# Gated linear attention and a low-rank mixer: two more batches in whole chunks, orders from a table, and the last batch's transposes on a DMA queue

## The chip, the cores and the metric

The kernel runs on one core of one Trainium2 chip. The metric is the device time of one execution, in microseconds; a kernel's time is the median over its runs. The engines are named as in the profile: PE (TensorE matmul), PEld (its weight loads), DVE (VectorE), ACT (ScalarE), POOL (GpSimd) and SP (SyncE, here the queue that issues DMA transfers).

## The reference

For 4 batches, 8 heads, 768 time steps and head dimension 48, a gated state is carried along time, and its output goes through a low-rank token mixer and an MLP:

```python
for t in range(S):                                   # S = 768, state is D x D per head, D = 48
    state = alpha[:, :, t, :, None] * state + np.einsum('bhd,bhe->bhde', k[:, :, t], v[:, :, t])
    y[:, :, t] = np.einsum('bhd,bhde->bhe', q[:, :, t], state)
x = y.transpose(0, 2, 1, 3).reshape(B, S, H * D)     # 4 x 768 x 384
h = x.transpose(0, 2, 1) @ U @ V                     # U: 768 x 32, V: 32 x 768
u = x + h.transpose(0, 2, 1)
out = u + np.maximum(u @ w_ch1, 0.0) @ w_ch2         # 384 -> 1536 -> 384
```

Inputs and output are float32; the kernel computes in bfloat16 with float32 sums.

## The kernel before

Each batch has three parts. The first computes the attention, in six units of 128 rows. Within a unit the decay is a running product of alpha: `lt` is the logarithm of alpha (ACT), a triangular matmul sums it along time into a PSUM bank, and two exponentials on ACT give `ai` (its inverse) and `aa`; a small third one gives `tot`, the decay over the whole unit. `rk = k * ai` and `rq = q * aa` are made on DVE or GpSimd, `rv` is a cast of v. PE transposes `rk` and `rq` (into PSUM, from where ACT or DVE copies them to `kT` and `qT`), multiplies them into scores, DVE masks the scores into `pm`, and PE adds the state's share (`qT` by the state `st`) to `pm` by `rv`. The result is copied to `xb`. The next state is made from `rk` by `rv`, the last state and `tot`.

There are two forms of unit. `stage_pair` (batches 0, 1 and 2, by `PAIR`) takes two chunks of 128 time steps together, but half of the heads: even and odd steps lie next to each other on a partition, so that a load (L342) moves runs of 96 floats. It works on blocks of 64 rows, with 16 small matmuls for the scores (L445), 16 for the masked product (L531), 8 for the state (L479), 4 for the state's share (L518), 8 transposes (L418) and 8 matmuls for the cumulative sum (L384 to L391). `stage_gla` (batch 3) takes one whole chunk of 128 steps and all heads: its load (L349) moves runs of 48 floats; it has 8 matmuls for the scores (L605), 8 for the masked product (L664), 4 for the state (L628), 4 for the state's share (L662), 8 transposes (L584) and 6 for the cumulative sum (L554 to L557).

The second part, `stage_mix`, applies the low-rank mixer (L681, L712) and transposes the result (L722) to `uT`. The third is the MLP: `mlp1` (L749, three matmuls of 384 columns per group, then a relu on ACT, L759, or DVE, L761, into `h1t`) and `mlp2` (L772, then an addition on DVE, L779, and a store, L780). The MLP of a batch is interleaved with the attention of the next one. At the start PE also runs matmuls on a tile of zeros (L291), wherever it would wait in the first 28 us.

The order is made when the program is built. Every step is recorded with `P.add`, with the engines that may run it and a cost for each, what it reads and writes, a priority, and a `slack`. `Plan.run` then simulates the engines with these costs and picks, step by step, the one that can start first; ties go by priority. It also hands out the buffers: input tiles come from a pool of 36 (`io`), and matmul results from the eight PSUM banks. What comes out is a fixed order for each engine. All transfers are issued on SP's queue: 96 input loads of 192 KB (four tensors, 24 units), 24 weight tiles (L317), two small ones and 24 stores. They take eight completion semaphores in turn, and a transfer is issued only when the one eight places before it has landed.

Of the kernel before, what the change touches and what calls it, by code (L numbers as in the profile page):

```python
# [11 lines left out]
ALU = mybir.AluOpType  # L12

# [23 lines left out]
class Op:  # L37
    __slots__ = ("engs", "fn", "prio", "deps", "bufs", "n", "users", "est", "i", "mode", "slack", "eng", "t")


class Plan:
# [4 lines left out]
    TOL = 150.0  # L46
# [10 lines left out]
    def add(self, engs, fn, r=(), w=(), prio=0.0, mode="F", slack=0.0, after=()):  # L57
        op = Op()
        op.engs, op.fn, op.prio, op.mode, op.slack = engs, fn, prio, mode, slack
# [17 lines left out]
        op.deps.discard(op)  # L77
        bufs = []
# [10 lines left out]
    def run(self):  # L89
        for op in self.ops:  # L90
            op.n = len(op.deps)
            for d in op.deps:
                d.users.append(op)
        ready = [op for op in self.ops if op.n == 0]
        clock = {}
        order = []
        dma = 0.0
        mode = "F"
        todo = len(self.ops)
        while todo:  # L100
            per = {}
            for op in ready:
                t = op.est
                for b in op.bufs:
                    if b.slot is None:
                        s = sorted(x for x in b.pool.free if x is not None)
                        if len(s) <= b.reserve:
                            t = None
                            break
                        t = max(t, s[b.reserve])  # L110
                if t is None:
                    continue
                at = {eng: max(t, clock.get(eng, 0.0)) for eng in op.engs}
                soon = min(at[eng] + c for eng, c in op.engs.items()) + self.TOL
                for eng, c in op.engs.items():
                    if at[eng] + c <= soon:
                        per.setdefault(eng, []).append((at[eng], op))
            best = None
            for eng, ok in per.items():
                t0 = min(t for t, _ in ok)  # L120
                t1, op = min(((t, o) for t, o in ok if t <= t0 + 1.0), key=lambda x: (x[1].prio, x[1].i))
                key = (t1, t1 + op.engs[eng])
                if best is None or key < best[0]:
                    best = (key, eng, op)
            if best is None:
                raise RuntimeError("the plan is stuck")
            (t, _), eng, op = best
            for b in op.bufs:
                if b.slot is None:
                    p = b.pool  # L130
                    _, x = min((f, x) for x, f in enumerate(p.free) if f is not None)
                    p.free[x] = None
                    b.idx, b.slot = x, p.slots[x]
            ready.remove(op)
            op.eng, op.t = eng, t
            cost = op.engs[eng]
            if eng == "SP":
                dma = max(dma, t + 600.0) + cost
                clock[eng] = max(t + 450.0, dma - 3500.0)
                end = dma + 2000.0  # L140
            else:
                if eng == "PE" and op.mode != mode:
                    cost += self.SWITCH
                    mode = op.mode
                clock[eng] = end = t + cost
            order.append(op)
            done = end + self.LAT[eng]
            for b in op.bufs:
                b.left -= 1
                b.last = max(b.last, done)  # L150
                if b.left == 0:
                    b.pool.free[b.idx] = b.last
            for u in op.users:
                u.n -= 1
                if eng == "PE" and "PE" in u.engs:
                    u.est = max(u.est, end)
                else:
                    u.est = max(u.est, done + u.slack)
                if u.n == 0:
                    ready.append(u)  # L160
            todo -= 1
        self.order = order
        self.clock = clock
        at = self.warm_from
        for op in order:
            if op.eng == "PE" and op.t < self.warm_until:
                n = int((op.t - at - 100.0) * self.warm_share / 216.0)
                for _ in range(n):
                    self.warm()
            if op.eng == "PE":  # L170
                at = op.t + op.engs["PE"]
            op.fn(op.eng)
# [7 lines left out]
def kernel(  # L180
# [33 lines left out]
    PAIR = (0, 1, 2)  # L214
    RES = (1, 1, 1, 0)
    P = Plan()
# [42 lines left out]
    nc.vector.memset(offd[64:128, :, 0], -30000.0)  # L259

# [54 lines left out]
    def weight(dst, src, key, prio, pr, engs):  # L315
        t = Buf(io)
        P.add({"SP": 540.0}, lambda e: nc.sync.dma_start(flat(t), src), w=[t], prio=prio)  # L317
# [17 lines left out]

    def stage_loads(b):
        def load(t, src, c, key):
            if b in PAIR:
                hs, sl = slice((c % 2) * HP, (c % 2 + 1) * HP), slice((c // 2) * 2 * C, (c // 2 + 1) * 2 * C)
                P.add(  # L340
                    {"SP": 750.0},
# [7 lines left out]
            P.add({"SP": 1000.0}, lambda e: nc.sync.dma_start(t(), src[b, :, sl, :].rearrange("h t d -> t h d")), w=[t], prio=key)  # L349

        for c in range(NC):
# [3 lines left out]
            for t, src, o in ((at, alpha, -0.7 if c else 0.0), (kt, k, 0.1), (qt, q, 0.2), (vt, v, 1.25 if c < NC - 1 and b in PAIR else 0.3)):  # L355
                load(t, src, c, kk + o)

    def xk(b, xb, c):
        return [(xb, c, 0), (xb, c, 1)] if b in PAIR else [(xb, c)]

    def stage_pair(b, u, sprev, xb):
# [3 lines left out]
        sl = 0.0 if b == 0 else 150.0  # L365
# [9 lines left out]
        P.add({"ACT": 435}, lambda e: nc.scalar.activation(jh(lt()[:, :, 0:D]), raw(at), AF.Ln), r=[at], w=[lt], prio=pr + 40, slack=sl)  # L375
        rv = Buf(rvs)
        P.add({"POOL": 480, "ACT": 420}, lambda e: copy(e, jh(rv()), raw(vt)), r=[vt], w=[rv], prio=pr + 20, slack=sl)
# [18 lines left out]
        P.add({"PE": mm(DM, Q, Q, 8, 4, 4, 4, 4)}, f_cum, r=[lt], w=[cb], prio=pr + 30, slack=sl)  # L396
        aa, ai, tot = Buf(aas), Buf(ais), Buf(tots)
        P.add({"ACT": 390}, lambda e: nc.scalar.activation(ai().rearrange("t h d -> t (h d)"), cb()[:, 0:DM], AF.Exp, scale=-1.0), r=[cb], w=[ai], prio=pr + 20, slack=sl)  # L398
        P.add({"ACT": 390}, lambda e: nc.scalar.activation(aa().rearrange("t h d -> t (h d)"), cb()[:, 0:DM], AF.Exp), r=[cb], w=[aa], prio=pr + 21, slack=sl)  # L399
        P.add({"ACT": 100}, lambda e: nc.scalar.activation(tot()[:, :, 0], cb()[:, DM : DM + 8], AF.Exp), r=[cb], w=[tot], prio=pr + 22, slack=sl)  # L400
# [7 lines left out]
        P.add(both, lambda e: f_scale(e, rk, kt, ai), r=[kt, ai], w=[rk], prio=pr + 10, slack=sl)  # L408
        P.add(both, lambda e: f_scale(e, rq, qt, aa), r=[qt, aa], w=[rq], prio=pr + 11, slack=sl)
# [20 lines left out]
        P.add({"PE": mm(*[C] * 4)}, lambda e: f_tr(rk, tk), r=[rk], w=[tk], prio=pr + 18, slack=sl)  # L430
        P.add({"PE": mm(*[C] * 4)}, lambda e: f_tr(rq, tq), r=[rq], w=[tq], prio=pr + 18, slack=sl)
        P.add({"DVE": 335, "ACT": 500}, lambda e: f_ev(e, kT, tk, False), r=[tk], w=[kT], prio=pr + 8, slack=sl)
        P.add({"DVE": 600, "ACT": 500}, lambda e: f_ev(e, qT, tq, True), r=[tq], w=[qT], prio=pr + 8, slack=sl)
# [17 lines left out]
        P.add({"PE": mm(*[C] * 4)}, f_sc, r=[kT, qT], w=[sc[0], sc[1]], prio=pr + 10, mode="Q", slack=sl)  # L451
# [6 lines left out]
        for par in range(2):  # L458
            P.add({"DVE": 605}, lambda e, par=par: f_mask(par), r=[sc[par]], w=[(pm, par)], prio=pr + 5, slack=sl)
# [26 lines left out]
        if onpe and sprev is not None:  # L486
            P.add({"PE": mm(Q)}, lambda e: f_id(e, 0, False), r=[(sprev, 1)], w=[db[0]], prio=pr + 8, slack=sl)
        P.add({"PE": mm(*[2 * D] * 4)}, f_d, r=[rk, rv], w=db, prio=pr + 8, mode="H", slack=sl)
        for c in range(nch):
# [10 lines left out]
            if onpe or prev is None:  # L500
                if onpe and c == 1:
                    P.add({"PE": mm(Q)}, lambda e: f_id(e, 1, True), r=[(st, 0)], w=[db[1]], prio=pr + 7, slack=sl)
                P.add({"DVE": 270}, lambda e, c=c, f=f_st: f(e, db[c]()[:, 0:Q]), r=[db[c], tot], w=[(st, c)], prio=pr + 4, slack=sl)
            else:
# [4 lines left out]
                    r=[db[c], prev], w=[sm], prio=pr + 4, slack=sl,  # L509
                )  # L510
                P.add({"POOL": 480, "DVE": 270}, lambda e, sm=sm, f=f_st: f(e, sm()[:, 0:Q]), r=[sm, tot], w=[(st, c)], prio=pr + 4, slack=sl)
# [24 lines left out]
        P.add({"PE": mm(*[2 * D] * 4, *[D] * 8) + 95}, f_y, r=[qT, rv, (pm, 0), (pm, 1)] + [x for x in before if x is not None], w=[yb[0], yb[1]], prio=pr, mode="H", slack=sl)  # L536
        for c in range(2):
            P.add({"ACT": 250, "DVE": 265}, lambda e, c=c: copy(e, xb()[:, 2 * blk + c, half * Q : (half + 1) * Q], yb[c]()[:, 0:Q]), r=[yb[c]], w=[(xb, 2 * blk + c, half)], prio=pr, slack=sl)
        return st

    def stage_gla(b, c, sprev, xb):
        kk = b * NC + c
        pr = kk * 100.0
        sl = 150.0
# [288 lines left out]
```

## Time and profile before

| | |
|---|---|
| time, median of 3 runs | 177.71 us (177.3 to 178.09) |
| span of the profiled execution | 175.2 us, which is 2.5 us under the median of the runs |
| PE busy | 165.0 us, 94% |
| DVE, ACT, POOL busy | 116.8, 104.9 and 52.9 us |
| PE clock granted | 1.000 throughout |
| chain that ended last, by engine | PE 62%, SP's queue 14%, DMA 14%, POOL 4% |
| loads, issue to landing | 4.5 us median (L342), 4.6 us (L349) |

How to read it: the span runs from the first to the last instruction of one profiled execution, and what lies around it is the difference to the time of a run. Busy time counts an engine's instructions, not its issuing of transfers. The chain that ended last is followed back from the last instruction, at each step to what released it. Rows of a line give durations as min/median/max. A mean of a matmul is its latency; how densely matmuls follow each other is read from the chain.

### The profile page before, as it was taken

What the parts mean: (1) busy time and instruction counts of PE and PEld (TensorE: products, weight loads), DVE (VectorE), ACT (ScalarE), POOL (GpSimd) and SP (SyncE); (2) the same over time, 40 slices, a digit from 0 to 9 for tenths busy, and PEclk for the clock granted to TensorE, in tenths of its full rate; (3) what the DMA queues carried; (4) which work ended last, traced back from release to release, by engine and by line L of the source; (5) the groups of instructions that cost most, each with busy time, mean ns of one, the idle gap of its engine ahead of it and who ended that gap; (6) DMA issues with size and microseconds to landing.
All of it is one profiled execution on the core that took longest, in us unless ns stands there. A gap on an engine that the chain in (4) does not pass through costs nothing.

```text
span 175.2 us, 5094 instructions
## 1 busy us (share of the span) xinstructions
PE 165.0 (94%) x1990; PEld 104.8 (60%) x1990; DVE 116.8 (67%) x251; ACT 104.9 (60%) x248; POOL 52.9 (30%) x92
## 2 busy tenths in 40 slices
PE   7788998699999999999999999999999999999992
PEld 2455665366566775766666666766666566666660
DVE  4588785398998889979888649987373385000321
ACT  4588874678788966457677434647784110996000
POOL 8055366258234432233243242920331000000000
PEclk9999999999999999999999999999999999999999
DMA  5999999999999999999698991021000212100222
GB/s 131 275 248 258 256 277 329 256 300 329 272 258 269 256 283 282 272 175 242 151 202 141 206 178 46 4 89 45 4 0 0 95 45 90 51 0 0 90 90 90
DMA packets 70744, 28.84 MB, mean 165 GB/s; under 512 B 64544, under 2 KB 70688, under 8 KB 70720
## 3 DMA queue, kind: packets, MB, share of 16 engines
q1 hardware_dynamic: 70720, 28.52, 67.2%
q8 instruction: 15, 0.25, 0.6%
q14 instruction: 9, 0.07, 0.2%
HBM read 23.79 MB, written 4.72 MB: 163 GB/s over the span
## 4 chain that ended last, share of the span: by engine, by line
PE 62%; SPq 14%; DMA 14%; POOL 4%; issue 3%; DVE 0%; POOLq 0%
PE ps L772 25%; PE ps L749 21%; SPq L342 11%; DMA io<-in_moe_w_ch_dram 6%; DMA io<-in_v_dram 5%; DMA io<-in_k_dram 3%; SPq L317 3%; POOL w_sb L302 2%; PE ps L418 2%; PE ps L712 2%; PE ps L722 2%; PE ps L584 2%; PE ps L531 1%; PE ps L445 1%; PE ps L605 1%
## 5 line engine op out<-in xcount | busy, mean ns | idle before, releaser
L749 PE MATMUL ps<-uT,w_sb 128*128 128x384 bf16 x288 | 53.5, 326 | 0.0
L772 PE MATMUL ps<-w_sb,h1t 128*128 128x384 bf16 x288 | 52.9, 326 | 0.0
L759 ACT ACTIVATE h1t<-ps 128x384 bf16<-128x384 f32 x70 | 33.9, 492 | 12.0 <-PE ps L749 11.9
L772 PEld LDWEIGHTS <-h1t 128*128 128x128 bf16 x288 | 26.1, 98 | 15.5 <-issue 0.6
L749 PEld LDWEIGHTS <-w_sb 128*128 128x128 bf16 x288 | 25.9, 98 | 15.4
L779 DVE TENSOR_TENSOR ou<-ub,ps 128x384 f32<-128x384 bf16 x24 | 13.2, 551 | 26.0 <-PE ps L772 25.8
L456 DVE TENSOR_TENSOR pm<-ps,maskp 128x512 bf16<-128x512 f32 x36 | 23.5, 682 | 2.8 <-PE ps L445 2.5
L761 DVE TENSOR_SCALAR h1t<-ps 128x384 bf16<-128x384 f32 x26 | 14.1, 553 | 7.6 <-PE ps L749 4.6
L302 POOL CAST rv<-io 128x384 bf16<-128x384 f32 x17 | 9.6, 567 | 28.2 <-DMA io<-in_v_dram 21.5
L298 ACT CAST xb<-ps 128x192 bf16<-128x192 f32 (+1 forms) x26 | 8.8, 353 | 10.3 <-PE ps L664 5.9
L298 ACT COPY qt<-ps 128x512 bf16<-128x512 bf16 x18 | 12.8, 709 | 3.5 <-PE ps L418 3.3
L375 ACT ACTIVATE lt<-io 128x384 bf16<-128x384 f32 x18 | 9.5, 527 | 8.3 <-DMA io<-in_alpha_dram 5.5
L713 DVE TENSOR_TENSOR ub<-xb,ps 128x384 bf16<-128x384 bf16 x24 | 12.0, 547 | 1.3 <-PE ps L712 1.3
L572 POOL TENSOR_TENSOR rk<-io,ai 128x384 bf16<-128x384 f32 x6 | 5.8, 970 | 22.6 <-ACT ai L565 22.6
L302 POOL CAST w_sb<-io 128x384 bf16<-128x384 f32 x21 | 10.6, 517 | 4.7 <-DMA io<-in_moe_w_ch_dram 4.4
L405 POOL TENSOR_TENSOR rk<-io,ai 128x384 bf16<-128x384 f32 x8 | 7.3, 915 | 11.6 <-ACT ai L398 10.8
L398 ACT ACTIVATE ai<-ps 128x384 bf16<-128x384 f32 x18 | 8.8, 487 | 2.1 <-PE ps L391 1.9
L298 ACT COPY kt<-ps 128x512 bf16<-128x512 bf16 x14 | 8.2, 583 | 1.8 <-PE ps L584 1.7
L615 DVE TENSOR_TENSOR pm<-ps,maskc 128x512 bf16<-128x512 f32 x12 | 7.9, 684 | 1.9 <-PE ps L605 1.8
L399 ACT ACTIVATE aa<-ps 128x384 bf16<-128x384 f32 x18 | 8.9, 493 | 0.0
L405 DVE TENSOR_TENSOR rk<-io,ai 128x384 bf16<-128x384 f32 x10 | 5.9, 588 | 4.1 <-ACT ai L398 4.1
L298 ACT COPY uT<-ps 128x768 bf16<-128x768 bf16 x4 | 3.2, 799 | 8.5 <-PE ps L722 8.3
(112 smaller groups left out, 256.8 us busy)
## 6 DMA issues: line engine op xcount, KB each, us to landing
io<-in_alpha_dram SPq DMA_DIRECT2D x24, 192.0 KB, 4.5
io<-in_k_dram SPq DMA_DIRECT2D x24, 192.0 KB, 4.5
io<-in_q_dram SPq DMA_DIRECT2D x24, 192.0 KB, 4.5
io<-in_v_dram SPq DMA_DIRECT2D x24, 192.0 KB, 4.6
io<-in_moe_w_ch_dram SPq DMA_DIRECT2D x24, 192.0 KB, 4.2
out_dram<-ou SPq DMA_DIRECT2D x24, 192.0 KB, 1.9
u_in<-in_moe_U_dram SPq DMA_DIRECT2D x1, 96.0 KB, 4.5
v_in<-in_moe_V_dram SPq DMA_DIRECT2D x1, 96.0 KB, 4.5
```

The costliest lines, as they stand in the source:

```text
L298: nc.scalar.copy(dst, src)
L302: nc.gpsimd.tensor_copy(dst, src)
L342: lambda e: nc.sync.dma_start(t().rearrange("p (h j) d -> p h (j d)", j=2), src[b, hs, sl, :].rearrange("h (p j) d -> p h (j d)", j=2)),
L375: P.add({"ACT": 435}, lambda e: nc.scalar.activation(jh(lt()[:, :, 0:D]), raw(at), AF.Ln), r=[at], w=[lt], prio=pr + 40, slack=sl)
L405: eng.tensor_tensor(jh(dst()[:, :, 0:D]), raw(a), jh(x()), op=ALU.mult)
L456: nc.vector.tensor_tensor(dst, s2, maskp.to_broadcast([C, 2, 2, C]), op=ALU.mult)
L713: P.add({"DVE": 465}, lambda e, c=c, hb=hb: nc.vector.tensor_tensor(ub()[:, c, :], xb()[:, c, :], hb()[:, 0:DM], op=ALU.add), r=[hb] + xk( ...
L749: nc.tensor.matmul(hb()[:, 0:TW], lhsT=w1_sb[:, ct, jt * 128 : (jt + 1) * 128], rhs=uT()[:, ct, tt * TW : (tt + 1) * TW], start=(ct == 0), ...
L759: nc.scalar.activation(dst, hb()[:, 0:TW], AF.Relu)
L761: nc.vector.tensor_scalar_max(dst, hb()[:, 0:TW], 0.0)
L772: nc.tensor.matmul(hb()[:, 0:DM], lhsT=h1()[:, jt, c * C : (c + 1) * C], rhs=w2_sb[:, jt, :], start=(jt == 0), stop=(jt == NJ - 1),)
L779: P.add({"DVE": 468}, lambda e: nc.vector.tensor_tensor(ou(), ub()[:, c, :], hb()[:, 0:DM], op=ALU.add), r=[hb, (ub, c)], w=[ou], prio=-100)
```

## The change

`PAIR = (0, 1, 2)` becomes `PAIRS = {0: 3, 1: 2, 2: 0, 3: 0}`: batch 0 stays in pairs, batch 1 has two thirds (four units) in pairs and its last two chunks whole, batch 2 and batch 3 are whole. So 10 units are pairs and 14 are whole chunks, instead of 18 and 6. Where batch 1 goes from pairs to whole chunks, the state comes from two tiles of the pairs, each with half of the heads.

In batch 3 (`QUEUE_T`), the transposes of `rk` and `rq` on PE and the copies from PSUM are replaced by `dma_start_transpose`, twelve of them, 128 KB each, from SBUF to SBUF, issued on ACT's queue. They take their turn among the same eight completion semaphores.

The whole chunk's cumulative sum loses one matmul, which kept the two head halves of `tot` apart; in its place the small exponential is made twice, each with a bias that leaves one half at zero, and not at all in the last chunk of a batch, which needs no next state.

The order on each engine, and the engine of each step, is no longer picked by `Plan.run` but read from `TABLE`, three characters a step (two for the step, one for the engine). `Plan.run` still hands out the buffers and places the fillers. So all orders change, those of batch 0 too: 52 instead of 70 relus are on ACT and 44 instead of 26 on DVE; 11 instead of 3 weight casts on ACT.

```diff
+CODE = "ABCDEFGHIJKLMNOPQRSTUVWXYZabcdefghijklmnopqrstuvwxyz0123456789+-"
+TABLE = """
+BASA9SA8SA4SA7SA6SA5SA+SA-SBISBESBMSBCSBBSCuADEACYABFSBKSBGSBDSBHSBJSCwPDGPCaPBOSBNSCxACZADHACzACbACdACcACyADJACeGCvGDIA
...
+"""
...
-    def run(self):
...
+    def run(self, table):
...
+        for n in range(0, len(table), 3):
+            op = self.ops[CODE.index(table[n]) * len(CODE) + CODE.index(table[n + 1])]
+            eng = {"P": "PE", "A": "ACT", "D": "DVE", "G": "POOL", "S": "SP"}[table[n + 2]]
...
-    PAIR = (0, 1, 2)
+    PAIRS = {0: 3, 1: 2, 2: 0, 3: 0}
     RES = (1, 1, 1, 0)
+    QUEUE_T = tuple((3, c) for c in range(6))
...
+    off = const.tile([C, 2], FP32, name="off")
+    nc.vector.memset(off, 0.0)
+    nc.vector.memset(off[64:128, 0:1], -30000.0)
+    nc.vector.memset(off[0:64, 1:2], -30000.0)
...
+    def paired(b, c):
+        return c // 2 < PAIRS[b]
...
             nc.tensor.matmul(cb()[:, 0:DM], lhsT=ut_ones, rhs=lt()[:, :, 0:D], start=True, stop=False)
-            nc.tensor.matmul(cb()[:, DM : DM + 2 * HP], lhsT=ident, rhs=offd.rearrange("p a b -> p (a b)"), start=False, stop=False)
             for p in range(HP):
                 nc.tensor.matmul(
-                    cb()[:, DM + 2 * p : DM + 2 * p + 2],
+                    cb()[:, DM + p : DM + p + 1],
                     lhsT=lt()[:, 2 * p : 2 * p + 2, :].rearrange("t h w -> t (h w)"),
-                    rhs=ones, start=False, stop=(p == HP - 1),
+                    rhs=ones[:, 0:1], start=False, stop=(p == HP - 1),
                 )
...
-        P.add({"ACT": 100}, lambda e: nc.scalar.activation(tot()[:, :, 0], cb()[:, DM : DM + 2 * HP], AF.Exp), r=[cb], w=[tot], prio=pr + 22, slack=sl)
+        for two in range(2 if c < NC - 1 else 0):
+            P.add({"ACT": 100}, lambda e, two=two: nc.scalar.activation(
+                tot().rearrange("p (a two) x -> p a (two x)", two=2)[:, :, two], cb()[:, DM : DM + HP], AF.Exp, bias=off[:, two : two + 1]
+            ), r=[cb], w=[(tot, two)], prio=pr + 22)
...
-        P.add({"PE": mm(*[C] * 4)}, lambda e: f_tr(rk, tk), r=[rk], w=[tk], prio=pr + 18, slack=sl)
-        P.add({"PE": mm(*[C] * 4)}, lambda e: f_tr(rq, tq), r=[rq], w=[tq], prio=pr + 18, slack=sl)
-        P.add({"DVE": 335, "ACT": 500}, lambda e: f_ev(e, kT, tk), r=[tk], w=[kT], prio=pr + 8, slack=sl)
-        P.add({"DVE": 335, "ACT": 500}, lambda e: f_ev(e, qT, tq), r=[tq], w=[qT], prio=pr + 8, slack=sl)
+        if (b, c) in QUEUE_T:
+            for dst, src in ((kT, rk), (qT, rq)):
+                P.add({"ACT": 100}, lambda e, dst=dst, src=src: nc.scalar.dma_start_transpose(dst(), src().rearrange("t h w -> t (h w)")), r=[src], w=[dst], prio=pr + 18, lag=2600)
+        else:
+            P.add({"PE": mm(*[C] * 4)}, lambda e: f_tr(rk, tk), r=[rk], w=[tk], prio=pr + 18)
+            P.add({"PE": mm(*[C] * 4)}, lambda e: f_tr(rq, tq), r=[rq], w=[tq], prio=pr + 18)
+            P.add({"DVE": 335, "ACT": 500}, lambda e: f_ev(e, kT, tk), r=[tk], w=[kT], prio=pr + 8)
+            P.add({"DVE": 335, "ACT": 500}, lambda e: f_ev(e, qT, tq), r=[tq], w=[qT], prio=pr + 8)
...
+                W = DM // len(sprev)
+                for n, (x, at0, key) in enumerate(sprev):
+
+                    def f_add(e, n=n, x=x, at0=at0):
+                        cs = slice(n * W, (n + 1) * W)
+                        old = x()[:, at0 : at0 + HP // len(sprev), :].rearrange("p a d -> p (a d)")
+                        nc.vector.tensor_tensor(sm()[:, cs], db()[:, cs], old, op=ALU.add)
...
-            if b in PAIR:
+            if paired(b, c):
                 st[c % 2] = stage_pair(b, c, st[c % 2], xb)
+                whole = [(x, 2, (x, 1)) for x in st if x is not None]
             else:
-                st[0] = stage_gla(b, c, st[0], xb)
+                x = stage_gla(b, c, whole, xb)
+                whole = [(x, 0, x)]
...
-    P.run()
-    global PLAN
-    PLAN = P
+    P.run("".join(TABLE.split()))
```

In the changed kernel the same steps stand some lines elsewhere: L340 for L342 and L347 for L349 (loads), L415 and L583 (transposes on PE), L594 (transposes on the queue), L608 (scores of a whole chunk), L759 and L769 (`mlp1` and its relu on ACT), L782 (`mlp2`), L789 and L790 (its addition and store).

## The prediction

> **What bounds the kernel now.** I read the page first, for the engine that is full and the slices in which it is not.
>
> ```profile
> PE 165.0 (94%) x1990; PEld 104.8 (60%) x1990; DVE 116.8 (67%) x251; ACT 104.9 (60%) x248; POOL 52.9 (30%) x92
> PE   7788998699999999999999999999999999999992
> PEclk9999999999999999999999999999999999999999
> ```
>
> PE is the full engine at an undisturbed clock; what it lacks is all in the first third. The table of stretches puts that into numbers (after the length: busy time of PE, weight loads, DVE, ACT, GpSimd; then clock, DMA share, GB/s).
>
> ```profile
> 0.00:62.30 62.30, 55.57 (x842) 35.39 (x844) 48.47 (x121) 45.12 (x111) 30.09 (x62) 1.00 1.07 266
> 62.30:100.00 37.70, 37.69 (x510) 24.03 (x510) 31.90 (x65) 24.59 (x58) 10.65 (x17) 1.00 1.02 215
> 100.00:140.00 40.00, 40.00 (x436) 26.07 (x435) 26.94 (x50) 22.42 (x55) 12.18 (x14) 1.00 0.22 54
> ```
>
> The chain that ended last says who made PE wait.
>
> ```profile
> 56.72 4.87 DMA io<-in_v_dram
> ...
> 62.27 0.35 PE ps L479 x8
> ...
> 148.35 11.70 PE ps L749 x72
> ```
>
> Up to 62.27 us the chain runs through SP's issues, landings and GpSimd's casts: loads set the pace, and PE idles 6.7 us. From there to the end it is PE alone. So PE work taken out after 62 us is worth its whole length, unless a new wait appears. The chain's pieces price such work: one unit of a pair and parts of a whole chunk.
>
> ```profile
> 88.16 0.17 PE ps L518 x4
> 88.33 0.30 PE ps L531 x16
> 89.72 0.27 PE ps L479 x4
> 89.99 0.56 PE ps L418 x8
> 92.01 0.35 PE ps L445 x16
> 94.38 0.17 PE ps L518 x4
> ...
> 118.55 0.45 PE ps L584 x8
> 119.48 0.17 PE ps L662 x4
> 119.65 0.20 PE ps L664 x8
> 120.34 0.33 PE ps L605 x8
> ```
>
> Last, the rows of the queue, since loads change shape (columns: min/median/max in ns).
>
> ```profile
> L342 SPq DMA_DIRECT2D io<-in_k_dram x18: 422/626/1346, 1.2 to 68.3; - x18
> L349 SPq DMA_DIRECT2D io<-in_k_dram x6: 384/882/1219, 72.4 to 97.2; - x6
> L780 SPq DMA_DIRECT2D out_dram<-ou x24: 332/332/1182, 60.1 to 172.4; - x24
> ```
>
> **Eight units become whole chunks (PE).** A pair unit recurs 6.22 us after the one before (L518 at 88.16 and 94.38). In between stand 24 L749 matmuls at 11.70/72 = 0.1625 us, 3.90 together; the unit is the other 2.3 (the five pieces shown 1.65, its cumulative sums 0.43 at 92.95, the rest switches between array shapes). A whole chunk costs 0.45 + 0.17 + 0.20 + 0.33, plus 0.17 for L628 and 0.27 for its cumulative sum, plus 0.11 by which the L772 group after L605 is stretched: 1.7. Eight times 0.6 is 4.9 us. Six of the eight are batch 2, which runs after 62 us, the other two lie at about 60 to 68: on PE's part of the chain.
>
> **Batch 3 without PE transposes.** Six chunks times 0.45 (L584 x8) is 2.7 us off PE, all after 100 us. With them go 7 PSUM copies on ACT (about 0.59 each, 4.1 us) and 5 on DVE.
>
> **The twelve transfers.** No trace row shows a transposing transfer; two things about it need bounds. *Hold*: how long ACT's in-order queue stands at each issue. SP's issues stand 0.33 (a store of 128 runs), 0.59 (L342, 512 runs) and 0.86 (L349, 1024 runs; both means of four medians). 128 rows in four blocks are nearest to 512 runs: I take 0.59, so 7.1 us in all, 3.0 more than the copies that leave; ends 0.33 and 1.1 (the longer L349 issues), so 4.0 to 13.2. What is queued behind is exactly what PE needs: the L769 relus that free PSUM banks, and the exponentials for the next chunks. ACT has 17.6 us idle in 100-140, so I let half of the 3.0 reach PE: 1.5 us; ends 0 and 9.1. A gain is excluded: PE waits for nobody for more than 0.2 us after 62 us, so freed banks buy nothing. *Landing*: the rows run from 1.9 us (stores) to 4.5 (loads). In the built order I count the PE work, at the pieces' prices, between each issue and the scores that read it; the smaller cover of each chunk is 2.8, 4.4, 6.4, 3.9, 6.5 and 3.1 us. At 1.9 nothing waits; at 4.5 it is 1.7 + 0.1 + 0.6 + 1.4 = 3.8 us. With few other transfers by then (share 0.22) the store is nearer: 0, the end 3.8 kept. The transfers also take their turn among eight completion semaphores: each waits on ACT until the DMA eight places earlier has landed, and batch 3's last v and q loads and several stores wait on SP for a transfer. Those stand in the covers above; if ACT runs late, they run late with it.
>
> [...]
>
> **The loads.** 32 loads (8 in batch 1, 24 in batch 2) go from 384-byte to 192-byte runs: 0.86 - 0.59 = 0.27 us more on SP each, 8.6 us together. Cover: SP itself waits for freed input slots, 12.1 us in 62-100 and 10.5 in 20-62 (its own waits, L342 and L349). Batch 2's 6.5 us fit into the first; gone, they would cost 6.5. The 8 early ones (2.2 us) lie where loads set the pace: between 0 and 2.2. In the built orders SP's issues have summed to 40.8 us when PE has 35.9 us of work behind it before, to 40.0 at 36.7 after; so nearly nothing, and I take 0.5.
>
> [...]
>
> **Other engines, and the order.** All 28 scalings of whole chunks go to GpSimd (0.94 each); with 10 instead of 15 of the pairs' it gets 10.5 us more, beside 27 idle in 62-100: 0, and at most 10.5 if that cover were gone. DVE loses 11 scalings (7 us) and takes 18 relus from ACT (10 us); at 31.9 of 37.7 it has no room for more, but that is about even. The small exponential is split in two, 0.2 us more on ACT a chunk. The relaid orders of the early stage can at best remove its 6.7 us of idle PE, and can as well lose as much; with loads in the lead there I take 0.
>
> **Sum.** 175.2 - 4.9 - 2.7 + 1.5 + 0.5 = 169.6 us of span. The three runs have a median of 177.71, which is 2.5 above the profiled span; kept: 172.1 us.
>
> **Rivals.**
> - *The queue's transposes land late (slower).* Place: the wait of the scores L608 on the transfer's semaphore, PE's order being fixed. With a landing of T the loss is the sum over chunks of T minus cover. It equals the 7.1 us of the other terms together at T = 5.3. The longest landing of a load is 5.9: 3.1 + 1.5 + 2.0 + 2.8 = 9.4, that is 175.2 - 7.1 + 9.4 = 177.5, and 180.0 us. For it: a landing was never seen here with another queue beside it, and ACT adds its wait for GpSimd's product. Against it: 1.9 for stores, and DMA share down at 0.22. Chance 0.20.
> - *Loads keep the chain until batch 1 ends.* All 2.2 are paid, batch 1's two units save nothing (1.2): 169.6 + 1.7 + 1.2 = 172.5, so 175.0 us. For it: the chain before 62 us and a DMA share of 1.07. Against: SP's slot waits. Chance 0.18.
> - *The new early orders remove half of PE's idle time:* 3.4 less, 168.7; up to 166 with no loss behind the transfers. Chance 0.07.
> - That the change does not do what it says is not among them: the built program has 1764 matmuls for 1990 and twelve transposing transfers on ACT.
>
> **The numbers.** The forecast has 0.55 (168 to 174.5). A measurement of this kernel tells some 0.5% from no change, 0.9 us. Faster: 0.55 + 0.07 + 0.13 of the loads' rival = 0.75. Within 0.5%: 0.05 of the loads' and 0.03 of the late transposes = 0.08. Slower: the other 0.17. Range 167 to 180: it leaves out some 0.05 below and 0.12 above.
>
> **What would show it.** Right: PE busy near 157 us, chain on PE from about 60 us, batch 3's stage with PE at 9 or more in every slice, transfers landing under 3 us, ACT's issues near 0.6 us, whole-chunk loads still near 0.86. Wrong: PE waiting on kt or qt (late transposes), ACT's relus or PE's L759 idle behind a transfer (hold), `in_..._dram` still in the chain after 66 us (loads), or DVE at the end of PE's waits.

## The result, and the profile after

The changed kernel takes 176.55 us (median of 6 runs, 175.94 to 178.59), the kernel before 177.55 us beside it. The ratio is 0.992, 95% interval 0.989 to 0.995: faster by 0.8%, not by the 3% that was forecast. One of the six runs, 178.59 us, had a lower clock on record (0.976) and is left out of the ratio; the quotient of the two medians is 0.994. The profiled execution took 176.57 us, its span is 174.9 us.

The page of the changed kernel, with the same rows as before:

```profile
PE 154.8 (89%) x1763; PEld 100.2 (57%) x1763; DVE 116.6 (67%) x252; ACT 87.0 (50%) x220; POOL 61.4 (35%) x100
PE   7968899999999999999999997587979999999800
PEclk9999999999999999999999999999999999999985
```

PE lost 10.2 us of work and the span 0.3. There are two new gaps: slices between 105 and 131 us, most with 5 to 8 tenths, and two empty slices at the end. The clock dips only in that end, where PE has nothing to do: 0.92 from 165 to 170 us and 0.50 from 170 us on (PE's last matmul ends at 165.5). The table of stretches of PE alone (length, busy time, clock, DMA share, GB/s):

```profile
0.00:100.00 100.00, 95.36 (x1267) 1.00 0.92 223
100.00:140.00 40.00, 33.91 (x335) 1.00 0.79 141
```

The idle time of the first 100 us fell from 6.7 to 4.6; between 100 and 140 us, where PE was full before, 6.1 us are idle. PE's waits from 95 to 145 us name who is late there:

```profile
PE ps L759 <- ACT h1t L769: 2.9, 2, 1.6
PE ps L608 <- DMA qt<-rq: 2.5, 2, 1.8
PE ps L608 <- DMA kt<-rk: 0.7, 2, 0.4
```

That is 2.9 us behind relus and 3.2 us behind landings. The rows of the transfers' line give the reason for both (min/median/max in ns, then issue to landing in us):

```profile
L594 ACTq DMA_TRANSPOSE kt<-rk x6: 1204/1222/1921, 102.0 to 125.2; - x6
L594 ACTq DMA_TRANSPOSE qt<-rq x6: 1206/1222/1286, 104.6 to 126.5; - x6
...
DMA to landing us min/median/max: 2.4/4.3/5.8
```

The second gap is in the chain that ended last. Before, it closed with PE's last matmul at 171.76 us and one addition; now:

```profile
157.08 7.81 PE ps L782 x48
...
164.92 0.56 DVE ou L789
...
165.50 1.83 DMA out_dram<-ou
...
167.42 0.57 DVE ou L789
...
168.01 1.83 DMA out_dram<-ou
...
169.96 1.02 DVE ou L789 x2
```

Two times an addition of the output waits until a store has landed. PE's own last matmul, four beyond the 48 of this chain, ends at 165.5 us by PE's timeline (156.91 + 8.61). So PE is done 6.2 us earlier than before, close to the 5.6 us of the forecast; but what follows it took 3.4 us before (175.2 - 171.76) and takes 9.4 us now.

### The profile page after: what moved, and what is told of

Its sections match the earlier page's. It is cut to its first block, busy times and chain, and to the rows that moved or that the text cites. A ratio compares the mean times of both kernels' runs of the same rounds, so it can differ in the third digit from the quotient of the medians.

```text
span 174.9 us, 4588 instructions
## 1 busy us (share of the span) xinstructions
PE 154.8 (89%) x1763; PEld 100.2 (57%) x1763; DVE 116.6 (67%) x252; ACT 87.0 (50%) x220; POOL 61.4 (35%) x100
## 3 DMA queue, kind: packets, MB, share of 16 engines
q10 hardware_dynamic: 6528, 1.57, 6.1%
## 4 chain that ended last, share of the span: by engine, by line
PE 67%; DMA 14%; DVE 7%; ACT 6%; ACTq 2%; issue 1%; SPq 1%; DVEq 0%
PE ps L782 24%; PE ps L759 21%; DMA qt<-rq 6%; DMA kt<-rk 3%; DMA io<-in_alpha_dram 2%; PE ps L722 2%; PE ps L583 2%; PE ps L608 2%; DMA out_dram<-ou 2%; ACTq L594 2%; PE ps L415 2%; PE ps L732 2%; ACT qt L293 2%; PE ps L675 1%; DVE ou L789 1%
## 5 line engine op out<-in xcount | busy, mean ns | idle before, releaser
L759 PE MATMUL ps<-uT,w_sb 128*128 128x384 bf16 x288 | 52.9, 326 | 2.9 <-ACT h1t L769 2.9
L782 PE MATMUL ps<-w_sb,h1t 128*128 128x384 bf16 x288 | 53.7, 326 | 0.0
L769 ACT ACTIVATE h1t<-ps 128x384 bf16<-128x384 f32 x52 | 24.4, 501 | 27.2 <-PE ps L759 22.6
L759 PEld LDWEIGHTS <-w_sb 128*128 128x128 bf16 x288 | 26.7, 98 | 18.9 <-issue 3.2
L782 PEld LDWEIGHTS <-h1t 128*128 128x128 bf16 x288 | 26.6, 98 | 16.7 <-issue 0.6
L771 DVE TENSOR_SCALAR h1t<-ps 128x384 bf16<-128x384 f32 x44 | 22.9, 551 | 16.9 <-PE ps L759 16.9
L618 DVE TENSOR_TENSOR pm<-ps,maskc 128x512 bf16<-128x512 f32 x28 | 18.1, 683 | 4.4 <-PE ps L608 4.3
L789 DVE TENSOR_TENSOR ou<-ub,ps 128x384 f32<-128x384 bf16 x24 | 12.8, 547 | 10.7 <-PE ps L782 6.6
L570 POOL TENSOR_TENSOR rq<-io,aa 128x384 bf16<-128x384 f32 x14 | 12.7, 912 | 20.5 <-issue 8.0
L293 ACT CAST xb<-ps 128x192 bf16<-128x192 f32 (+1 forms) x21 | 8.1, 407 | 13.4 <-PE ps L675 10.5
L453 DVE TENSOR_TENSOR pm<-ps,maskp 128x512 bf16<-128x512 f32 x20 | 12.8, 680 | 0.0
L293 ACT COPY qt<-ps 128x512 bf16<-128x512 bf16 x10 | 6.7, 716 | 4.4 <-PE ps L583 3.5
L642 POOL TENSOR_TENSOR st<-sm,tot 128x384 bf16<-128x384 f32 x5 | 4.1, 829 | 12.3 <-DVE sm L658 12.3
L658 DVE TENSOR_TENSOR sm<-ps,st 128x384 f32<-128x384 f32 (+1 forms) x10 | 5.1, 514 | 5.0 <-PE ps L631 4.2
L297 POOL CAST w_sb<-io 128x384 bf16<-128x384 f32 x13 | 6.3, 521 | 4.4 <-DMA io<-in_moe_w_ch_dram 4.4
L608 PE MATMUL ps<-qt,kt 48*128 48x128 bf16 x112 | 5.0, 218 | 3.2 <-DMA qt<-rq 2.5
```

The lines of the kernel that those rows point to most:

```text
L293: nc.scalar.copy(dst, src)
L297: nc.gpsimd.tensor_copy(dst, src)
L453: nc.vector.tensor_tensor(dst, s2, maskp.to_broadcast([C, 2, 2, C]), op=ALU.mult)
L570: eng.tensor_tensor(dst()[:, :, 0:D], a(), x(), op=ALU.mult)
L608: nc.tensor.matmul(sc[par]()[:, p * C : (p + 1) * C], lhsT=kT()[o : o + D, p, :], rhs=qT()[o : o + D, p, :], start=(p == 0), stop=(p == HP ...
L618: nc.vector.tensor_tensor(pm()[:, :, par, :], s2, maskc.to_broadcast([C, HP, C]), op=ALU.mult)
```

## Experiments

The theory after this reading: PE's saving came as forecast or better and is lost in two places, 6.0 us behind the last matmul, by the order of additions and stores and the four output slots, and 6 us in batch 3's stage, by the transposing transfers. Ratios are against runs of the kernel before on the same chip, with 95% intervals; the changed kernel stands at 0.992.

**The end: more slots, or another order.** In the changed order the stores of two chunks of batch 2 stand on SP behind the first store of batch 3, and so hold two of the four `ou` slots. Three of the six last additions take turns in one slot, each behind the store of the one before. `slots6` adds two slots, `tail` leaves four and moves steps.

```diff
-    outs = Pool(slots("ou", 4, [C, DM], FP32))
+    outs = Pool(slots("ou", 6, [C, DM], FP32))
```

> The changed kernel with six output slots instead of four; orders untouched. Theory (the last additions wait for output slots whose stores have not landed): of the two 2 us waits of the additions at the end one disappears, since only the last two additions still take a slot again; last addition ends near 168.5 instead of 171.0, so about 2.5 us less, 174.1 us. Rival (the stores' own traffic, or the clock below 1 in the last 15 us, sets the end): no change, 176.6 +- 0.5 us.

Measured 175.58 us, ratio 0.984 (0.978 to 0.990); 1.5 us below the changed kernel by the ratios. One of the two waits is gone, as expected, and PE's end has not moved; the chain's end:

```profile
165.41 1.84 DMA out_dram<-ou
...
167.34 0.45 DVE ou L789
...
167.84 0.56 DVE ou L789
```

The span fell by 3.2 us to 171.7; the runs scatter from 173.42 to 177.83, so its size is less sure than its sign.

```diff
+        moved = [x for x in self.ops if x.last]     # additions of batch 3, stores of batches 1 to 3
+        plan = [x for x in plan if not x[0].last]
+        for x in moved:                             # each right behind the last step that it needs
+            place = {y[0]: k for k, y in enumerate(plan)}
+            plan.insert(max(place[d] for d in x.deps) + 1, (x, engs[x]))
```

> The changed kernel with the additions of the last batch moved in the order to right behind their last group of matmuls, and the stores of batches 1 to 3 right behind their additions; still four slots. Theory (the end is lost to the place of additions and stores in the table): what follows the last matmul falls from 10.0 us to the 3.4 us of the kernel before, so 6.6 less, 170.0 us, with the last matmul still near 165. Rival (stores' traffic or the clock): 176.6 +- 0.5 us. Second rival (additions put earlier on VectorE delay the relus that PE waits for): the last matmul moves out by 1 us or more.

Measured 172.33 us, ratio 0.969 (0.965 to 0.973). VectorE's timeline at the end shows additions that wait for PE and no longer for a store:

```profile
162.09 0.55 DVE L800 TENSOR_TENSOR ou<-ub,ps 128x384 f32<-128x384 bf16 x1 [3.34 <-PE ps L793]
163.39 1.20 DVE L800 TENSOR_TENSOR ou<-ub,ps 128x384 f32<-128x384 bf16 x2 [0.75 <-PE ps L793]
165.34 1.85 DVE L800 TENSOR_TENSOR ou<-ub,ps 128x384 f32<-128x384 bf16 x3 [0.75 <-PE ps L793]
```

From the last matmul (166.60 by PE's timeline) to the end of the span it is now 3.9 us. The median gained 4.1 us on the changed kernel by the ratios, not the 6.6 expected: the last matmul came 1.1 us later. In this execution the clock was 0.83 from 110 to 120 us, while PE waited for transfers (4.0 us instead of 3.2); that the moved additions delayed relus is not what its waits show (1.7 us behind relus instead of 2.9).

**Batch 3: hold or landing.** First the transfers on the other queue:

```diff
-nc.scalar.dma_start_transpose(dst(), ...)
+nc.sync.dma_start_transpose(dst(), ...)
```

> The changed kernel with the twelve transposing transfers issued on SyncE's queue at the same places of the order. Theory A (the 1.22 us for which ScalarE stands at each issue is what costs PE time, through relus and exponentials that stand behind): ACT gets 14.7 us free, PE's idle time in 100 to 130 us falls from 6.0 to 3 or less, 3 us less, 173.6 us. Theory B (it is the 4 us of landing): the scores wait as before, 176.6 +- 0.7 us. Rival (SyncE, standing at waits for GpSimd's products and at its own issues, delays the last loads of q and v and the stores): slower by 1 us or more.

Measured 184.14 us, ratio 1.037 (1.032 to 1.042): the rival. SP's queue is not free: at these places of the order it stands behind the last loads. The first transfer is issued at 114.5 us instead of 102.0, and PE sits in one wait:

```profile
PE ps L608 <- DMA qt<-rq: 12.4, 1, 12.4
```

So this run could not tell hold from landing. The others do. `pe_b3` takes the transfers out:

```diff
-            for dst, src in ((kT, rk), (qT, rq)):
-                P.add({"ACT": 100}, ... nc.scalar.dma_start_transpose(...))
+            P.add({"PE": mm(*[C] * 8)}, f_both, r=[rk, rq], w=[tb])    # eight transposes into one bank
+            P.add({"ACT": 590}, f_out, r=[tb], w=[kT, qT])             # kT copied on VectorE, qT on ScalarE
```

> The changed kernel with batch 3's q and k transposed on PE again: eight transposes of a chunk into one bank at the place of its second transfer, one copy out on VectorE and one on ScalarE two PE groups later; all else as in the table. Theory (hold and landing of the transfers together make the 6.0 us of idle PE in 100 to 130 us): PE busy 2.7 us more, idle 6.0 less, 3.3 us less, 173.3 us. Rival (the idle time comes from the table's order and the load of the other engines): 2.7 us more, 179.3 us, with PE idle as before in 100 to 130 us.

Measured 174.08 us, ratio 0.980 (0.976 to 0.984). `pe_hold` keeps PE's transposes and issues the transfers too, into tiles that nobody reads:

> The kernel of the run pe_b3, and beside its PE transposes the twelve transposing transfers are issued on ScalarE's queue as well, into spare tiles that nobody reads; so the hold of ScalarE is there and the landing is waited for by nobody. Theory A (the hold of 1.22 us, 14.7 together, delays relus, exponentials and copies that PE waits for): PE idle in 100 to 130 us rises from 0.7 to 3 or more, 3 us more than pe_b3's 174.1, 177.1 us. Theory B (only the landing cost PE time): within 0.7 us of 174.1.

Measured 177.16 us, ratio 0.995 (0.993 to 0.998). `pe_plain` differs from it in one call:

```diff
-nc.scalar.dma_start_transpose(d(), ...)
+nc.scalar.dma_start(d().rearrange("p e c -> p (e c)"), ...)
```

> As the run pe_hold, but the twelve unread transfers are plain copies of the same tiles (128 rows of 1024 bytes) on ScalarE's queue, not transposing ones. Theory (what costs is the 1.22 us for which ScalarE stands while a transposing transfer is issued): a plain issue stands near the stores' 0.33 to 0.6 us, 4 to 7 us together instead of 14.7, PE idle in 100 to 140 us rises by 1 us or less, 174.1 to 175 us. Rival (it is the wait for GpSimd's products and for landings on ScalarE's in-order queue, whatever the transfer's kind): as pe_hold, 177 us, PE idle 3.7 in 100 to 140 us.

Measured 173.57 us, ratio 0.979 (0.975 to 0.982): no cost that can be seen. PE's stretch from 100 to 140 us in the three, in the order `pe_b3`, `pe_hold`, `pe_plain` (busy time second; the changed kernel has 33.91):

```profile
100.00:140.00 40.00, 39.29 (x411) 1.00 0.46 106
```

```profile
100.00:140.00 40.00, 36.26 (x383) 1.00 0.81 149
```

```profile
100.00:140.00 40.00, 39.30 (x411) 1.00 0.57 143
```

And the issues, of `pe_hold` and then of `pe_plain`:

```profile
L633 ACTq DMA_TRANSPOSE spare<-rk x6: 1205/1229/1860, 103.0 to 126.7; - x6
...
  ACT h1t L812: 4.1, 2
...
DMA to landing us min/median/max: 2.4/4.5/6.5
```

```profile
L633 ACTq DMA_DIRECT2D spare<-rk x6: 472/521/558, 102.3 to 122.3; - x6
...
DMA to landing us min/median/max: 2.0/3.3/5.1
```

Same places in the same queue, same tiles, same waits for GpSimd's products: only the transposing kind costs. It stands 1.22 us instead of 0.52, and relus wait behind it (L812, 4.1 us). The transposing kind is also more traffic (DMA share 0.81 instead of 0.57 in the stretches above), but PE's two longest waits in `pe_hold` are on relus and none is on a load:

```profile
PE ps L576 <- ACT h1t L812: 1.5, 1, 1.5
PE ps L674 <- ACT h1t L812: 1.3, 1, 1.3
```

So the hold costs PE 3.0 us (39.3 - 36.3), as the 2.9 us of relu waits in the changed kernel said, and the remaining 3 of its 6 us are the landings, as its 3.2 us of waits on `qt` and `kt` said.

**Without the table.** The scheduler of the kernel before orders the new steps, once with `QUEUE_T = ()` (whole chunks alone, batch 3 transposed on PE), once with the transfers:

> The whole chunks alone: batch 2's six units and batch 1's last two as whole chunks, batch 3 transposed on PE, and the order from the scheduler of the kernel before, not from the table. Theory (the whole chunks' saving on PE of 4.9 us reaches the end when additions and stores follow as in the kernel before): 0.5 lost to the loads, 4.4 less than before, 173.1 us (ratio 0.975), 3.4 us behind the last matmul. Rival (192-byte loads or GpSimd's scalings take the saving): ratio 0.99 or more, with PE waiting for loads or GpSimd after 62 us.

> Whole chunks and the twelve transfers on ScalarE's queue, with the order from the scheduler of the kernel before in place of the table. Theory (the transfers cost more PE waiting than the 2.7 us of transposes they take off PE, in any order): 2 to 3 us above greedy_whole, 176 us (ratio 0.99), PE idle in batch 3's stage. Rival (it is the table's order that makes the transfers late): 2.7 us below greedy_whole, 170.4 us (ratio 0.96).

The whole chunks alone measured 170.0 us, ratio 0.955 (0.950 to 0.959). PE is busy for 160.2 us, 4.8 less than before, waits for nothing from 62 us on, and the end is the old one, one addition behind the last matmul. That is 3.1 us better than expected: the loads cost nothing, and PE's idle time in the first 100 us fell by 1.9 us (to 4.9) on top of the saving. With the transfers it is 183.85 us, ratio 1.028 (1.021 to 1.035), where 176 was expected; the waits of its PE from 60 us on are one line:

```profile
PE ps L620 <- DMA qt<-rq: 12.3, 6, 2.8
```

Each of the six chunks waits some 2 us for its transfer, although the median landing is 2.5 us here and was 4.3 in the changed kernel: by these numbers this order leaves little PE work between issue and scores. So the transfers lose in either order, and the table made them cheaper: its places leave 3.2 us of such waits instead of 12.3.

**Both repairs.**

> Both repairs at once: batch 3's q and k transposed on PE as in the run pe_b3, additions and stores of the end placed behind their matmuls as in the run tail. Theory (two separate losses, one in batch 3's stage, one behind the last matmul): they add, last matmul at 161.3 and 3.6 us behind it, 6.3 us less than pe_b3's 174.1, 167.8 us. Rival (the additions placed earlier on VectorE delay the relus and cost PE the 1.7 us by which the last matmul came later in the run tail): 169.5 us.

Measured 168.08 us (167.67 to 168.76), ratio 0.944 (0.940 to 0.948), the fastest version. The last matmul ends at 162.77 us (154.16 + 8.61 by PE's timeline) and the span 3.4 us later. The two losses are separate: by the ratios it is 6.4 us below `pe_b3`, as expected. The last matmul came 1.5 us later than expected and 0.9 later than in `pe_b3`. That is not the rival's delayed relus, for PE waits for none; its busy time is 1.3 us higher than in `pe_b3`, of which the fillers (the matmuls on zeros) make 1.2 (7.3 us instead of 6.1).

## Why the prediction was off

The direction and the range held, the size did not: 176.55 us instead of 172.1. By its own steps, for the profiled execution (174.9 of span instead of 169.6):

- **What failed: the sum ends at PE's last matmul.** It took over the 3.4 us behind it without a term, on "From there to the end it is PE alone", though the order of all additions and stores was to change. They cost 6.0 us more, the largest error. The built order had it to be read: two stores of batch 2 behind one of batch 3, three additions in one slot, and six additions bunched behind the last groups.
- **Landing: 0 taken, 3.2 us measured**, near the upper end of 3.8. The store's 1.9 us was chosen because the DMA share had been 0.22 in this stage. In the changed order it is 0.79: whole-chunk loads are issued until 116.4 us (99.3 before), and the transfers add their own traffic (without them, in `pe_b3`, it is 0.46). The median landing was 4.3 us, the load's row and not the store's; in `sp_issue`, where the transfers are issued behind the last loads, it was 2.4, with a share of 0.45 from 120 to 130 us and 0.42 from 130 to 140. The turns at the semaphores are in the trace too: on SP three loads waited 4.3 us in all for the landing of a transfer (L347, 2.2 behind `qt` and 2.1 behind `kt`). The covers were right: with 4.3 us they give 3.1. The late-transposes rival had the right place; its 5.3 us was not reached by the median. That figure, and the 180.0 us at 5.9, left out the 1.5 us of hold: with it the gain is used up at 5.0 us, and 5.9 gives 181.5.
- **Hold: 0.59 us taken, 1.22 measured**, outside the ends of 0.33 and 1.1. The nearest rows gave the right price for a plain transfer of these tiles (0.52) and no price for a transposing one. On PE the hold was 2.9 us instead of 1.5. "Half reaches PE" was too much: of 10.5 us extra on ACT (12 x 1.22 less 4.1 of copies) 2.9 arrived. One thing the sum did not count is in the trace: ACT works on beside an issue at times; five of its instructions start during the one from 102.04 to 103.34 us. The price too low and the share too high partly cancel, which was luck.
- **Eight units to whole chunks: 4.9 us taken, 4.8 measured** in `greedy_whole` (5.1 without the fillers). The 0.2 us of a pair unit that was put down to switches between array shapes stands behind the matmuls on 64 and 48 rows in the chain of before: six L749 take 1.08 us behind L531 and three 0.59 behind L445, where 0.1625 each makes 0.98 and 0.49.
- **Batch 3's transposes: 2.7 us taken.** PE busy is 1.9 us higher in `pe_b3` than in the changed kernel.
- **Loads: 0.5 us taken, nothing lost.** The whole-chunk loads stood 0.71 us on SP (mean of four medians) and the pairs' 0.53: 0.18 more each, not 0.27. PE's idle time in the first 100 us fell by 2.1 us, and it is as low in `greedy_whole` (4.9), so the whole chunks and not the table brought it.
- **Orders: 0 taken.** The table takes some 2 us off PE's busy time (158.0 us in `pe_tail`, 160.2 in `greedy_whole`), and 3.6 us without the fillers, which are 7.3 and 5.9 us of these; which neighbours do it is open. Then it loses 6.0 at the end.

The balance of the span: +6.0 (end) + 3.2 (landing) + 1.4 (hold) - 0.5 (loads) - 2.1 (early idle time) - 2.6 (PE busy 154.8 instead of 157.4) = 5.4, against 5.3 measured. What lies around the span was 1.7 us and not the 2.5 that was kept: in the later runs of the kernel before it is 1.7 to 1.8 us too, so the execution in the trace of before was some 0.8 us faster than the median.

## What to carry to other kernels

When the order of a kernel is rewritten, sum up to the last store and not to the last matmul: look in the built order for who frees each output slot, and for old stores that stand behind new ones. Moving PE's transposes to a DMA queue traded 0.45 us of PE per chunk here for two holds of ScalarE's queue, 1.22 us each, and a landing of 4.3 us (medians). Price the hold by a run of that very kind of transfer (the rows of other kinds had said 0.59), and the landing at the DMA share of the new order, not of the old (0.79 here and not 0.22). An unread copy of a transfer, beside the old path, measures what it costs without its landing (3.0 us of PE in `pe_hold`).

## What the runs showed of the hardware

- A transposing transfer of 128 x 512 bfloat16 within SBUF held the queue of its issuing engine for 1.20 to 1.24 us (medians), on ScalarE's queue (`greedy_queue` 1.21 and 1.23, `pe_hold` 1.23 and 1.21) and on SyncE's (`sp_issue` 1.24 and 1.20) alike; a plain copy of the same tile 0.52 us (`pe_plain`).
- It landed 2.4 us after the issue at the earliest (plain: 2.0). The median was 4.3 us in the changed kernel and 4.5 in `pe_hold` (DMA share from 100 to 140 us 0.79 and 0.81; plain, in `pe_plain`: 3.3 at 0.57), and 2.5 in `greedy_queue` (share 0.49) and 2.4 in `sp_issue`. At the same places of the queue, `pe_hold` against `pe_plain`, the transposing transfers landed 0.4 (earliest) to 1.2 us (median) later.
- The twelve transposing transfers of the changed kernel took 6528 packets, 1.57 MB and 6.1% of 16 engines' span; by estimate (6.1% of 174.9 us over twelve) 0.89 us of all DMA engines each. The DMA share from 100 to 140 us was 0.46 in `pe_b3`, 0.81 with the unread transposing transfers (`pe_hold`) and 0.57 with the plain copies (`pe_plain`); by estimate (the differences to 0.46, times 40 us, over twelve) 1.2 and 0.4 us each, with whatever else moved in the stretch.
- In `sp_issue` the granted clock fell while PE had nothing to do, to a mean of 0.62 from 110 to 120 us, and was back at 1.00 only in the stretch from 130 us (columns: length, PE, weight loads, DVE, ACT, POOL; clock, DMA share, GB/s):

```profile
110.00:120.00 10.00, 0.00 (x0) 0.00 (x0) 0.00 (x0) 0.51 (x2) 0.71 (x1) 0.62 0.89 205
120.00:130.00 10.00, 8.05 (x67) 4.91 (x68) 3.81 (x7) 3.60 (x11) 2.42 (x5) 0.70 0.45 67
```

The clock was still 0.70 in the stretch where PE worked again. If its low value was 0.50, as in the last 4.9 us of the changed kernel, the two means put it at about 112.4 to 126 us by estimate, some 4 us into PE's new work. By the chain, the first scores behind the wait took 1.03 us (L608 x16 at 121.95), the next ones, at clock 1.00, 0.55 (at 130.89): this wait of 12.4 us cost more than its length.
